# An attention and MLP kernel: MLP products as four of 32 columns, and scores in runs of three

## The chip, the core and the metric

The kernel runs on one core of a Trainium2 chip. TensorE (PE) multiplies, ScalarE (ACT) computes the exponentials and tanh, VectorE (DVE) does the elementwise work, GpSimd (POOL) and SyncE (SP) start most of the remaining transfers. The metric is the device time of one execution in microseconds, the median of a few runs.

## What is computed

From `x` (1, 2048, 640): a layer norm without weights, then two branches on it, multi-head attention (32 heads of 20 columns) and an MLP (640 to 1536 to 640, tanh gelu), both added to `x`.

```python
xn = _layernorm(x, axis=-1)
return x + _A_ref(xn, A_wqkv, A_wo) + _B_ref(xn, B_w1, B_b1, B_w2, B_b2)
...
scores = jnp.einsum("bhqd,bhkd->bhqk", q, k) * (Dh ** -0.5)
p = _softmax(scores, axis=-1)
o = jnp.einsum("bhqk,bhkd->bhqd", p, v)
...
y = _layernorm(x, axis=-1)
h = _gelu(jnp.einsum("bsd,df->bsf", y, w1) + b1)
return jnp.einsum("bsf,fd->bsd", h, w2) + b2
```

## The kernel before

All is computed in float32 accuracy from 16-bit pieces: an operand is split into a high and a low half, and a product is three passes (high by high, high by low, low by high; `PASS`).

**Stages.** First the norm, the transposes, the projections to queries, keys and values, and the splitting of the weights (up to 224 us). Then one long loop over attention, with the MLP laid between its parts, and at the end the output projection, whose first products also go into the loop when the results they need are there.

**The loop.** Heads go in pairs `g` (16 of them), the tokens of the queries in halves `hf` and quarters `cc` of 512 columns, the keys in 16 blocks `kb` of 128. `ORDER` runs through 32 pairs (g, hf); the last four g go through hf 0 first and hf 1 afterwards. For each key block:

- `scores` (L742, the products recorded at L748): two products, one for each head of the pair, with 61 rows each, at rows 0 and 64 of the array, into a PSUM tile `s` of 128 x 1024. The pool `psS` has three such tiles. ScalarE's exponential (L750) reads it and writes `p` in float32; `p` has seven buffers, `low` four.
- Half of the key blocks (`SPLIT` is 1, 1, 0, 0 and so on) have their values in 16-bit pieces. For these `rest` (L757) has VectorE subtract the upper half of `p` from `p` (L762), into `low` in f16; the value products then read the upper half as bf16, and `low`. For the other blocks `p` is multiplied as it is, in f32.
- `pv` (L767) does the value products, of 32 columns each (`product`, L778 and L779). Four quarters `q` of the array's columns write to four strips of 32 partitions of `o`. They accumulate over 16 key blocks; then ScalarE copies `o` to `ev` (L800).

**The order in the loop.** A group is four key blocks. It is written out by hand: scores of two blocks, a part of the MLP, scores of two blocks, the value products of the group before (the scores of the next two blocks follow). `tick` (L689) lets every side job (gelu, the sums behind the attention, loads) take one step after each run of two. `other` (L1186) doles out the MLP: each call adds `rate` = 1.265 us to a credit, and a unit of the MLP is cut in as many parts as its cost asks for.

**The MLP.** `chain` gives units: `layer1` (L1021, products at L1031: weights 128 x 128, 256 moving columns; a unit has 30, for two of the 12 blocks of hidden features) and `layer2` (L1053, products at L1061: 128 x 128 with 320 moving columns; 36 in a unit). They write to `psM`, one PSUM buffer, which the projection `z` (L1146) uses too. After a layer-1 unit `gelu` (L961) runs over several ticks: two VectorE steps, a third, ScalarE's tanh (L977), and three more on VectorE, which write `hT`.

**The end.** `finish` (L861) sums the two parts of a group of heads, divides by the sums and writes `oscr`. For the last heads it goes a shorter way: the sums are spread with small products `rb` (L931), and VectorE multiplies and splits (L942 to L944). `projection` (L1121) loads a piece of 256 tokens from `oscr` (`load_piece`, L1089) when all heads of these tokens are written (`known`), then does 15 products for each 128 tokens and 320 columns. After the loop, `more` (L1233) goes on with the projection, a tick after every three products.

Of the kernel before, what the change touches and what calls it, by code (L numbers as in the profile page):

```python
# [34 lines left out]
CHUNK = 1.75  # L35
# [9 lines left out]
def mha_mlp_kernel(tc, x, wqkv, wo, w1, b1, w2, b2, out):  # L45
# [4 lines left out]
    with (  # L50
# [617 lines left out]
        with ExitStack() as scope:  # L668
# [72 lines left out]

            def scores(g, hf, cc, kb):  # L742
# [24 lines left out]
            def pv(units):  # L767
# [240 lines left out]
            xs, hTs = {}, {}  # L1008
            unscaled = []
# [11 lines left out]
            def layer1(mc, f):  # L1021
# [4 lines left out]
                for i in range(2):  # L1026
                    n = 0
                    fo_ = (f + i) % 4 * P
                    for k in range(KD):
                        for a, b in PASS:  # L1030
                            nc.tensor.matmul(ps[:, i], w1v[:, k, (f + i) // 4, a, fo_ : fo_ + P], xnt[:, k, b, :],  # L1031
                                             start=(n == 0), stop=(n == 3 * KD - 1))
# [20 lines left out]
            def layer2(mc, j, hf):  # L1053
# [5 lines left out]
                for f in range(KF):  # L1059
                    for a, b in PASS:  # L1060
                        nc.tensor.matmul(ps[:, :320], hTs[mc][:, f, a, j * P : (j + 1) * P],  # L1061
                                         w2v[:, f, b, hf * 320 : (hf + 1) * 320],
                                         start=(n == 0), stop=(n == 3 * KF - 1))
# [112 lines left out]
            with tc.manual_schedule():  # L1176
# [3 lines left out]
                rate = 1.265  # L1180
                groups = [(g, hf, cc, kb) for g, hf in ORDER for cc in range(2) for kb in range(0, NKB, GRP)]
                prev = None

                runs = []

                def other():  # L1186

                    nonlocal credit
                    if not runs:
                        unit = next(fill)  # L1190
                        if unit is None:
                            credit = 0.0
                            return
# [6 lines left out]
                for g, hf, cc, kb0 in groups:  # L1200
                    units = []
                    for kb in range(kb0, kb0 + GRP):
                        units.append([g, hf, cc, kb, scores(g, hf, cc, kb)])
                        if kb % 2 == 0:
                            continue
                        reading[0] = kb % GRP > 1 and prev is not None and prev[-1][3] == NKB - 1
                        tick()
                        if kb % GRP == 1:

                            rest(units[0])
                            credit += rate
                            other()
                        else:
                            for u in units[1:]:
                                rest(u)
                            if prev:
                                pv(prev)
                            else:  # L1220

                                credit += rate
                                other()
                    prev = units
# [21 lines left out]
                pv(prev)  # L1246
# [96 lines left out]
```

## Time and profile before

| | us |
|---|---|
| median of three runs | 1337.81 (1336.13 to 1339.84) |
| span of the profiled execution | 1337.9 |
| loop, first score product to the last | 224.7 to 1270.5 |
| PE busy | 1325.8 |
| ACT busy | 1128.0 |
| DVE busy | 1055.1 |

The page lists busy time by engine, the share of it in 40 slices of the span, the chain of work that ended last, and the costliest groups of instructions. In a row of groups stand line, engine, operation, tiles, shapes and count, then busy time in us and the mean of one in ns, then the engine's idle time before them and who ended it. In a row of the timeline stand the start, the time from the first start to the last end, and the count of instructions merged into it; TensorE's products overlap, so the time that a block holds the engine is read from start to start. `q` behind an engine's name marks its queue, where it issues transfers.

### The profile page before, as it was taken

The numbers are of one execution on the slowest core, as the hardware profiler recorded it, in microseconds if no ns is written. First come the engines' busy times: TensorE is split into PE (matmuls) and PEld (weight loads), VectorE is DVE, ScalarE is ACT, GpSimd is POOL, SyncE is SP. The second block draws the span as 40 slices with busy tenths as digits, with TensorE's granted clock in tenths as the row PEclk, the third lists the DMA queues.
The fourth block names the chain that finished last, engine by engine and source line by source line (L and its number), as shares of the span: only waits on it lengthen the run. The fifth ranks groups of instructions, "written<-read, shape, count | busy, mean of one in ns | idle before, by whom it ended". The sixth has DMA issues, their size and how long they took to land.

```text
span 1337.9 us, 29042 instructions
## 1 busy us (share of the span) xinstructions
PE 1325.8 (99%) x11635; PEld 586.7 (44%) x11635; DVE 1055.1 (79%) x1431; ACT 1128.0 (84%) x1306; POOL 37.5 (3%) x86
## 2 busy tenths in 40 slices
PE   9999899999999999999999999999999999999998
PEld 6645456444434343434343443344443434333366
DVE  7656754998788989878897879888879888997742
ACT  7844334999999999999999999999999999999900
POOL 3010000000000000000000000000000000000000
PEclk9999899999999999999999999999999999999999
DMA  9778723021203232212322132223032323334375
GB/s 279 254 196 176 136 79 104 15 59 39 66 28 103 61 83 81 63 48 59 111 63 81 33 93 66 75 69 94 19 80 71 93 66 87 118 95 118 105 218 188
DMA packets 100326, 129.54 MB, mean 97 GB/s; under 512 B 24292, under 2 KB 66664, under 8 KB 100188
## 3 DMA queue, kind: packets, MB, share of 16 engines
q1 hardware_dynamic: 96652, 120.25, 31.6%
q0 software_dynamic: 2912, 6.90, 2.8%
q8 instruction: 92, 1.51, 0.5%
q10 hardware_dynamic: 624, 0.51, 0.1%
q14 instruction: 46, 0.38, 0.1%
HBM read 82.14 MB, written 42.51 MB: 93 GB/s over the span
## 4 chain that ended last, share of the span: by engine, by line
PE 87%; DVE 6%; DMA 4%; ACT 1%; issue 1%; SPq 0%; ACTq 0%; DVEq 0%
PE o L779 30%; PE s L748 20%; PE py L1061 13%; PE pu L1031 11%; PE z L1146 5%; PE qkp L337 5%; PE vp L410 3%; DVE low L762 2%; DMA xt<-in_A_x_dram 1%; DMA xnt<-row 1%; DMA qkscr<-qkhl 1%; DVE st L255 1%; DVE qkhl L353 1%; ACT p L750 1%; DMA wos<-in_A_wo_dram 0%
## 5 line engine op out<-in xcount | busy, mean ns | idle before, releaser
L750 ACT ACTIVATE p<-s 128x1024 f32<-128x1024 f32 x1024 | 973.9, 1050 | 33.1 <-PE s L748 27.1
L762 DVE TENSOR_TENSOR low<-p 128x1024 f16<-128x1024 f32 x512 | 614.3, 1218 | 144.8 <-ACT p L750 144.0
L779 PE MATMUL o<-p,vfull 128*32 128x512 bf16 (+1 forms) x4096 | 429.0, 493 | 0.0
L748 PE MATMUL s<-qs,ks 61*128 61x512 f16 x2048 | 311.4, 381 | 0.2 <-ACT p L750 0.2
L748 PEld LDWEIGHTS <-ks 61*128 61x128 f16 x2048 | 61.2, 94 | 278.4 <-issue 276.1
L1061 PE MATMUL py<-w2t,hT 128*128 128x320 f16 x1152 | 178.5, 300 | 0.0
L1031 PE MATMUL pu<-xm,w1t 128*128 128x256 f16 x1440 | 178.2, 273 | 0.1
L1031 PEld LDWEIGHTS <-w1t 128*128 128x128 f16 x1440 | 131.0, 98 | 64.0 <-issue 50.2
L1061 PEld LDWEIGHTS <-hT 128*128 128x128 f16 x1152 | 102.3, 98 | 88.1 <-issue 53.9
L337 PE MATMUL qkp<-xnt,wv 128*128 128x512 f16 x600 | 131.1, 379 | 1.3 <-issue 1.3
L779 PEld LDWEIGHTS <-vfull 128*32 128x32 f16 x3072 | 59.9, 95 | 138.4 <-issue 106.9
L779 PE MATMUL o<-low,vfull 128*32 128x512 f16 x1024 | 101.3, 377 | 0.1
L337 PEld LDWEIGHTS <-wv 128*128 128x128 f16 x600 | 58.2, 98 | 71.0 <-issue 1.6
L779 PEld LDWEIGHTS o<-p,vfull 128*32 128x32 f32 x2048 | 61.7, 108 | 53.2
L410 PE MATMUL vp<-wv,xnt 128*128 128x320 f16 x480 | 69.5, 306 | 3.7 <-DVE qkhl L353 3.7
L1146 PE MATMUL z<-w1t,ot 128*128 128x320 f16 x480 | 67.4, 299 | 0.0
L352 ACT ACTIVATE qkhl<-qkp,qks 128x1024 f16<-128x1024 f32 (+1 forms) x24 | 23.1, 964 | 46.3 <-PE qkp L337 26.6
L410 PEld LDWEIGHTS <-xnt 128*128 128x128 f16 x480 | 47.9, 100 | 23.8 <-issue 3.7
L1146 PEld LDWEIGHTS <-ot 128*128 128x128 f16 x480 | 46.0, 98 | 22.9 <-issue 5.5
L353 DVE SCALAR_TENSOR_TENSOR qkhl<-qkp,qks,qkhl 128x1024 f16<-128x1024 f32 (+1 forms) x24 | 26.5, 1104 | 32.9 <-ACT qkhl L352 32.9
L1103 DVE SCALAR_TENSOR_TENSOR acc<-z,sc,acc 128x320 f32<-128x320 f32 x32 | 17.5, 549 | 37.3 <-PE z L1146 37.2
L800 ACT ACTIVATE ev<-o 128x512 f32<-128x512 f32 x64 | 39.5, 618 | 2.2 <-PE o L779 2.1
(195 smaller groups left out, 670.4 us busy)
## 6 DMA issues: line engine op xcount, KB each, us to landing
qkscr<-qkhl SPq DMA_DIRECT2D x40, 256.0 KB
opart<-ev SPq DMA_DIRECT2D x124, 80.0 KB
ks<-qkscr SPq DMA_DIRECT2D x120, 80.0 KB
qs<-qkscr SPq DMA_DIRECT2D x192, 40.0 KB
oa<-opart SPq DMA_DIRECT2D x32, 240.0 KB
xt<-in_A_x_dram SPq DMA_DIRECT2D x16, 320.0 KB
xscr<-xnt SPq DMA_DIRECT2D x4, 1280.0 KB
xm<-xscr SPq DMA_DIRECT2D x8, 640.0 KB
```

The lines of the kernel that those rows point to most:

```text
L337: nc.tensor.matmul(ps[:, i, :], wv[:, k, q, a, mm * P : (mm + 1) * P], xnts[c][:, k, b, :], start=(k + n == 0), stop=(k == KD - 1 and n == 2))
L352: nc.scalar.activation(hl[:, 0, i0:i1], ps[:, i0:i1], AF.Copy, scale=a)
L353: nc.vector.scalar_tensor_tensor(hl[:, 1, i0:i1], ps[:, i0:i1], a, hl[:, 0, i0:i1], ALU.mult, ALU.subtract)
L410: nc.tensor.matmul(ps[:, hf, :320], xnts[c][:, k, a, j * P : (j + 1) * P], wv[:, k, 2, b, hf * 320 : (hf + 1) * 320], start=(n == 0), stop ...
L748: nc.tensor.matmul(ps[:, a, :], ks[64 * a : 64 * a + 61, kb * P : (kb + 1) * P], qs[64 * a : 64 * a + 61, cc * 512 : (cc + 1) * 512], star ...
L750: nc.scalar.activation(pt, ps, AF.Exp, scale=QS)
L762: nc.vector.tensor_sub(low, pt, upper(pt))
L779: nc.tensor.matmul(pv.o[32 * q : 32 * q + 32, :], src[:, v0 - PAD * (1 - q % 2) :][:, :32], t, start=q not in pv.begun, stop=last, skip_gr ...
L800: nc.scalar.activation(evs[g, hf][:, cc], pv.o, AF.Copy)
L1031: nc.tensor.matmul(ps[:, i], w1v[:, k, (f + i) // 4, a, fo_ : fo_ + P], xnt[:, k, b, :], start=(n == 0), stop=(n == 3 * KD - 1))
L1061: nc.tensor.matmul(ps[:, :320], hTs[mc][:, f, a, j * P : (j + 1) * P], w2v[:, f, b, hf * 320 : (hf + 1) * 320], start=(n == 0), stop=(n == ...
L1146: nc.tensor.matmul(ps[:, :320], ot[:, k, a, j * P : (j + 1) * P], wov[:, k, b, h * 320 : (h + 1) * 320], start=(n == 0), stop=(n == 3 * KD ...
```

## The change

1. The products of both MLP layers go through `quarters`: each product of 128 columns becomes four of 32 columns, one per strip of 32 output partitions, with the same moving operand. The projection's products stay as they are.
2. The loop goes over sets of eight key blocks. Scores come in runs of three, three and two. After each run comes a part of the MLP, and right behind it value products: after the first run those of the last four key blocks of the set before, after the second those of blocks 0 and 1, after the third those of blocks 2 and 3.
3. `other` is called after each run, with the shares 0.65, 1.46 and 0.52 us, and cuts a unit accordingly, at whole steps (three products of layer 1 or of the projection, two of layer 2).
4. `pv` does the f32 blocks before the split ones, not after.
5. `rest` is called after the first run for blocks 0 and 1, after the third for blocks 4 and 5; after the second run `tick` is called a second time. A gelu that isn't done when the next begins is run to its end first (`latest`).

```diff
-CHUNK = 1.75
+RUNS = (3, 3, 2)
+SHARE = (0.65, 1.46, 0.52)
...
+            def quarters(o, w, t, **kw):
+
+                for r in range(0, P, 32):
+                    nc.tensor.matmul(o[r : r + 32], w[:, r : r + 32], t, skip_group_check=True, **kw)
...
                 of32 = lambda kb, a: PAD + kb * VROW + (2 * g + a) * VW
+                for a in range(2):
+                    for n, (kb, pt) in enumerate(whole):
+                        product(2 * a + n % 2, vfull, of32(kb, a), pt[:, a])
                 for kb, up, _ in split:
...
-                for a in range(2):
-                    for n, (kb, pt) in enumerate(whole):
-                        product(2 * a + n % 2, vfull, of32(kb, a), pt[:, a])
...
-                            nc.tensor.matmul(ps[:, i], w1v[:, k, (f + i) // 4, a, fo_ : fo_ + P], xnt[:, k, b, :],
-                                             start=(n == 0), stop=(n == 3 * KD - 1))
+                            quarters(ps[:, i], w1v[:, k, (f + i) // 4, a, fo_ : fo_ + P], xnt[:, k, b, :],
+                                     start=(n == 0), stop=(n == 3 * KD - 1))
...
-                                    begin(gelu(ps, r2f, hTs[mc], f))
+                                    if latest and latest[0] in sides:
+                                        sides.remove(latest[0])
+                                        for _ in latest[0]:
+                                            pass
+                                    latest[:] = [gelu(ps, r2f, hTs[mc], f)]
+                                    begin(latest[0])
...
-                        nc.tensor.matmul(ps[:, :320], hTs[mc][:, f, a, j * P : (j + 1) * P],
-                                         w2v[:, f, b, hf * 320 : (hf + 1) * 320],
-                                         start=(n == 0), stop=(n == 3 * KF - 1))
+                        quarters(ps[:, :320], hTs[mc][:, f, a, j * P : (j + 1) * P],
+                                 w2v[:, f, b, hf * 320 : (hf + 1) * 320],
+                                 start=(n == 0), stop=(n == 3 * KF - 1))
...
-                rate = 1.265
...
+                    credit += SHARE[turnno % 3]
                     if not runs:
...
-                        k = max(round((cost - credit) / rate) + 1, math.ceil(cost / CHUNK))
-                        runs.extend(n * (i + 1) // k - n * i // k for i in range(k))
+                        lens = []
+                        have = credit
+                        while not lens or (cost - have > 0.5 * SHARE[(turnno + len(lens)) % 3] and len(lens) < n):
+                            if lens:
+                                have += SHARE[(turnno + len(lens)) % 3]
+                            lens.append(have)
+                        lens = [max(0.0, v) for v in lens]
+                        cuts = [round(n * v / lens[-1]) for v in lens] if lens[-1] > 0 else [n]
+                        runs.extend(y - x for x, y in zip([0] + cuts, cuts))
...
+                flow = [(g, hf, cc, kb0) for g, hf in ORDER for cc in range(2) for kb0 in range(0, NKB, 8)]
+                held = []
+                for g, hf, cc, kb0 in flow:
                     units = []
-                    for kb in range(kb0, kb0 + GRP):
-                        units.append([g, hf, cc, kb, scores(g, hf, cc, kb)])
...
+                    for r, n in enumerate(RUNS):
+                        for _ in range(n):
+                            kb = kb0 + len(units)
+                            units.append([g, hf, cc, kb, scores(g, hf, cc, kb)])
+                        reading[0] = r == 0 and kb0 == 0 and bool(held)
                         tick()
...
+                        other()
+                        if r != 1:
+                            for u in units[4:6] if r else units[:2]:
+                                rest(u)
                         else:
...
+                            reading[0] = False
+                            tick()
+                        if r == 0:
+                            if held:
+                                pv(held)
+                        else:
+                            pv(units[2 * r - 2 : 2 * r])
+                    held = units[4:]
```

More of the change, by code (lines that the diff above doesn't have):

```diff
@@ L1008, in mha_mlp_kernel @@
             xs, hTs = {}, {}
+            latest = []
             unscaled = []
@@ L1179, in mha_mlp_kernel @@
                 credit = 0.0 - next(fill)
-                rate = 1.265
-                groups = [(g, hf, cc, kb) for g, hf in ORDER for cc in range(2) for kb in range(0, NKB, GRP)]
-                prev = None
                 runs = []
+                turnno = 0
                 def other():
-                    nonlocal credit
+                    nonlocal credit, turnno
+                    credit += SHARE[turnno % 3]
                     if not runs:
@@ L1197, in other @@
+                        lens = [max(0.0, v) for v in lens]
+                        cuts = [round(n * v / lens[-1]) for v in lens] if lens[-1] > 0 else [n]
+                        runs.extend(y - x for x, y in zip([0] + cuts, cuts))
                     for _ in range(runs.pop(0)):
                         credit -= next(fill)
-                for g, hf, cc, kb0 in groups:
+                    turnno += 1
+                flow = [(g, hf, cc, kb0) for g, hf in ORDER for cc in range(2) for kb0 in range(0, NKB, 8)]
@@ L1207, in mha_mlp_kernel @@
                         tick()
[L1208 to L1214, printed above, removed]
-                        else:
[L1216 to L1223, printed above, removed]
```

7 lines of the change are left out of this document (2 added, 5 removed).

## The prediction

> **What bounds the kernel now.** I read the page first: the span, the busy shares, the chain that ended last.
>
> ```profile
> span 1337.9 us, 29042 instructions
> PE 1325.8 (99%) x11635; PEld 586.7 (44%) x11635; DVE 1055.1 (79%) x1431; ACT 1128.0 (84%) x1306; POOL 37.5 (3%) x86
> PE 87%; DVE 6%; DMA 4%; ACT 1%; issue 1%; SPq 0%; ACTq 0%; DVEq 0%
> L750 ACT ACTIVATE p<-s 128x1024 f32<-128x1024 f32 x1024 | 973.9, 1050 | 33.1 <-PE s L748 27.1
> ...
> L748 PE MATMUL s<-qs,ks 61*128 61x512 f16 x2048 | 311.4, 381 | 0.2 <-ACT p L750 0.2
> ```
>
> TensorE carries the chain. The average hides stages, so next came the loop alone, from the first score product to the last (busy times by stretch: length, then PE, PEld, DVE, ACT, POOL, each with its count, then the granted clock):
>
> ```profile
> 224.70:1271.00 1046.30, 1045.89 (x9791) 419.75 (x9794) 892.66 (x1064) 1013.00 (x1134) 13.58 (x16) 1.00 0.26 72
> ```
>
> PE has no gap in 1046 us; ScalarE is at 97% of it. A gain on PE is thus worth its full size only until ScalarE stands in the way. How PE spends the loop, and what ScalarE needs, shows in the timeline:
>
> ```profile
> 602.84 0.60 PE L748 MATMUL s<-qs,ks 61*128 61x512 f16 x4
> 603.38 1.16 PE L1031 MATMUL pu<-xm,w1t 128*128 128x256 f16 x9
> 604.47 0.61 PE L748 MATMUL s<-qs,ks 61*128 61x512 f16 x4
> 605.00 0.64 PE L779 MATMUL o<-p,vfull 128*32 128x512 bf16 x8
> 605.47 0.39 PE L779 MATMUL o<-low,vfull 128*32 128x512 f16 x4
> 605.68 1.03 PE L779 MATMUL o<-p,vfull 128*32 128x512 f32 x8
> 606.64 0.60 PE L748 MATMUL s<-qs,ks 61*128 61x512 f16 x4
> ...
> 611.01 1.48 PE L1031 MATMUL pu<-xm,w1t 128*128 128x256 f16 x12
> 612.43 0.60 PE L748 MATMUL s<-qs,ks 61*128 61x512 f16 x4
> ...
> 624.06 1.26 PE L1061 MATMUL py<-w2t,hT 128*128 128x320 f16 x8
> 625.25 0.61 PE L748 MATMUL s<-qs,ks 61*128 61x512 f16 x4
> ...
> 627.97 1.53 PE L1061 MATMUL py<-w2t,hT 128*128 128x320 f16 x10
> 629.43 0.61 PE L748 MATMUL s<-qs,ks 61*128 61x512 f16 x4
> ```
>
> ```profile
> 603.27 3.77 ACT L750 ACTIVATE p<-s 128x1024 f32<-128x1024 f32 x4 [0.17 <-PE s L748]
> 606.90 0.63 ACT L800 ACTIVATE ev<-o 128x512 f32<-128x512 f32 x1
> 607.38 7.49 ACT L750 ACTIVATE p<-s 128x1024 f32<-128x1024 f32 x8
> ```
>
> From start to start, 9 products of layer 1 hold PE 1.09 us (603.38 to 604.47) and 12 hold it 1.42. Three more cost 0.33, so 0.109 each, and 1.09 - 9 x 0.109 = 0.107 is a fixed price of the block. Layer 2: 1.19 for 8, 1.46 for 10, so 0.135 each and 0.11 over. A run of two key blocks' scores takes 0.54, again 0.107 plus 2 x 0.216. Inside the value products, which change from bf16 to f16 to f32, the steps of 0.46, 0.21 and 0.96 hold one such price, at the end (0.96 = 0.855 + 0.107). So PE pays 0.107 us whenever the shape of the array's tiles changes, not when the type does. For ScalarE: four exponentials in 603.27 to 606.90, so 0.907 us apart, 1.05 long; the first starts 0.43 after its run of scores does.
>
> **The change, part by part.**
>
> *Changes of shape.* By the order of the built programs, the loop before has 1023 blocks of one shape on PE (512 of scores, 254 of value products, 257 of the MLP and projection); the changed one has 792 (384 of scores, 383 of 32 columns, 25 of projection, which stays 128 wide). 231 blocks x 0.107 = **-24.7 us**.
>
> *Quarters.* 1440 + 1152 products become four each, so 7,776 more matmuls and as many weight loads. What a quartet costs is shown by the one other place of this shape with short moving rows:
>
> ```profile
> 56.22 0.52 PE L382 MATMUL norms<-sq,heads 128*32 128x128 bf16 x24
> 56.67 1.09 PE L299 MATMUL pt<-ident,xt 128*128 128x128 f32 x8
> ...
> 93.19 0.41 PE L382 MATMUL norms<-sq,heads 128*32 128x128 bf16 x16
> 93.52 0.39 PE L114 MATMUL mxp<-acc,ones 128*128 128x5 f32 x2
> ```
>
> 24 of them hold PE 0.45 us, 16 hold it 0.33: eight more take 0.12 (a rounding of 0.01 either way), so a quartet with 128 columns takes 0.055 to 0.065, loads included, and one with 256 should take 0.11, as the whole product does. The 16-bit value quartet (605.47, 0.21 for 512 columns) says the same. The bf16 quartets (0.46 for two) are 0.015 dearer; at that price 2592 quartets would add 39 us. I take 0: the MLP's operands lie dense in 16 bits, as those of the 0.21 row do. Ends: -5 and +39.
>
> *Three score buffers, runs of three.* The scores' tiles still rotate through three buffers. With runs of two, the second key block of a run waits for an exponential of an earlier run that ended long ago. With runs of three, the third block waits for the last exponential of the run before (after a run of two, too). With t the start of a run of three, m the MLP time in a run: its last exponential ends at t + 0.43 + 2 x 0.907 + 1.05 = t + 3.29. PE reaches the next run's third block at t + 0.755 (three blocks of scores) + m + 1.64 (f32 0.855, bf16 0.465, f16 0.215, change 0.107) + 0.43. So PE waits if m is under 0.47 in the first run of a set of eight key blocks, and by the same sum (0.54 + m + 0.96 + 0.43 against 0.43 + 0.907 + 1.05) if m is under 0.46 in the third. In the second run, with its shorter value products, m under 1.18 makes ScalarE late by the difference. The built program's chunks, over 128 sets: first run 0.52 to 0.81 in 116, 0.33 or less in 6; third run 0.54 in 47, 0.65 in 42, 0.33 or less in 19; second run 1.31 or more in 106. These small chunks cost 19 x 0.14 + 6 x 0.14 and 21 sets with a light second run some 3: together 6.5 us. Then the 48 tanh, which ScalarE runs between exponentials:
>
> ```profile
> L977 ACT ACTIVATE w<-w 128x512 f32<-128x512 f32 x48 | 32.0, 666 | 0.0
> L800 ACT ACTIVATE ev<-o 128x512 f32<-128x512 f32 x63 | 38.9, 618 | 0.1
> L966 DVE TENSOR_TENSOR u<-pu,r2f 128x512 f32<-128x512 f32 x48 | 32.8, 683 | 0.2
> ```
>
> A tanh takes 0.52 of ScalarE's time (0.666 less the 0.14 by which exponentials overlap, 1.05 - 0.907). Twenty stand behind a second run: the next exponentials are late by 1.18 + 0.52 - 1.33 = 0.37, of which the third run's spare (0.54 or 0.65 less 0.46) hides 0.14; 20 x 0.23 = 4.6. Nineteen stand behind a third run, where most is hidden: 1.5; nine behind a first: 0.5. The 63 copies of o (0.48) fall where ScalarE waits for PE anyway: 0. Sum of waits **+13 us**; ends 0 (where a wait already taken relieves the next, and more is hidden) and +28 (a slower hand-over, below).
>
> *VectorE and the single buffer of the MLP.* A unit's first product waits until VectorE has read the unit before (0.68, L966). PE's time between the MLP parts of two runs shrinks from at least 2.7 (604.47 to 607.18) to 0.465 + 0.215 + 0.107 + 0.54 = 1.33 after a second run. Latency and 0.68 fit if VectorE, 85% busy in the loop, is free: some 40 ends of units x 0.05, **+2 us**; ends 0 and 8. The sums and lows that are moved wait on nothing new that is late: the latest `low` is emitted in the third run and used at the end of the next first run, over 4 us on.
>
> *The tail.* The shares add up to 2.63 per eight blocks, where 2 x 1.265 were given before, so the loop takes 165 projection products, not 66. That work is only moved. But these are the rows of the first half of the tokens, which now cover the wait for the last heads:
>
> ```profile
> 1274.99 9.55 PE L1146 MATMUL z<-w1t,ot 128*128 128x320 f16 x69
> ...
> 1284.46 2.50 PE L931 MATMUL rb<-lt,sel 64*80 64x64 f32 x32
> ...
> 1286.90 39.70 PE L1146 MATMUL z<-w1t,ot 128*128 128x320 f16 x291
> ...
> 1288.80 0.67 DVE L942 TENSOR_TENSOR oa<-oa,rb 80x512 f32<-80x512 f32 x1
> ...
> 1290.69 2.10 ACTq L945 DMA_DIRECT2D oscr<-oa  x2
> ...
> 1293.98 1.03 SPq L1097 DMA_DIRECT2D ot<-oscr  x2
> ```
>
> Before, 339 products follow `rb` (291 + 48), 99 of them of the first half: 13.6 us of cover. In the changed order 240 follow, all of the second half: no cover. What is late then: VectorE's three steps (1288.80 to 1290.69, 1.9), the write of `oscr` until its reader may start (to 1293.98, 3.3), the load of `ot` (two of 320 KB: landed by 1300.5, when PE uses it without a wait, so 1.03 to 6.5; I take 4.4). PE stands still for 9.6 us, and then the clock drops, as it did here:
>
> ```profile
> 159.50 1.76 PE L410 MATMUL vp<-wv,xnt 128*128 128x320 f16 x6 [3.67 <-DVE qkhl L353]
> 158.10:164.90 6.80, 5.40 (x21) 3.08 (x21) 6.43 (x16) 0.72 (x1) 0.00 (x0) 0.50 0.75 178
> ```
>
> A gap of 3.7 us led to 5.4 us of work at half clock, 2.7 lost. Together **+12.3 us**; ends +6 and +15.
>
> *Sum.* -24.7 + 0 + 13 + 2 + 12.3 = +2.6, of which I take off 1 because waits of the ring and of VectorE partly fall together: 1337.9 + 1.6 = **1339.5 us**, against the profiled execution's span, which is that of the median (1337.81). The measurement tells 0.3% (4 us) from no change.
>
> **Rivals.**
>
> *Faster.* The ring hardly waits, since each wait gives the next runs slack, and `ot` lands early: -24.7 + 3 + 0 + 9 = -12.7, **1325 us**. For it: ScalarE's own need in the loop is 1024 x 0.907 + 48 x 0.52 + 63 x 0.48 = 984 us, 37 less than the 1021 left to PE. Against: slack in the mean does not help a run whose buffer is taken.
>
> *The ring locks.* Place: the third scores of every run of three. The margins above are 0.07 to 0.19 us, at a hand-over from ScalarE to PE taken as zero. From 0.15 us on, the 78 runs with chunks of 0.54 wait too, and all others longer: some 16 us more, **1356 us**. For it: PE waited only 0.2 us for ScalarE in the loop before, so no row shows the hand-over. Against: the exponential's 1.05 may contain it.
>
> *PE's instruction supply.* The loop then issues 9791 + 7776 = 17,567 matmuls in 1,020 us, 58 ns each, where before it was 107. Place: PE's queue, in the MLP parts. It decides from the point where PE's instruction stream gives a matmul and its load less often than every 58 ns; each ns more costs 17.6 us, so 3 ns add 53: with the tail's 12 **1403 us**. The rows bound it only loosely: 24 pairs in 0.45 us (a burst that can have waited in a queue) on the one side, 107 ns and +860 us on the other; I take the burst's side. [...]
>
> *The change does not do what it says:* the quarters run one after another, 7,776 x 0.109 = +850 us. The rows of `norms` speak against it.
>
> **How the numbers follow.** Forecast 0.45 (its own range 1331 to 1348: 0.09 faster, 0.19 within 0.3%, 0.17 slower); faster 0.28; the ring locks 0.15; supply 0.10; in series 0.02. Faster 0.09 + 0.28 = 0.37, same 0.19, slower 0.44. The range reaches from the best ends (-24.7 + 0 + 6 + waits of 3) to the ring that locks with some dearer quartets: 1321 to 1360; supply and series, 0.12, and a part of the edges are left out.
>
> **What would show it.** Right: fewer and longer blocks on PE, 0.11 us per layer-1 quartet; some 10 us of waits of `s` on ScalarE where before were 0.2; one gap of 8 to 11 us behind `rb` and a second stretch at clock 0.5. Wrong: a quartet above 0.12 (or gaps on PE that nothing but issue ends) raises the time at once, 2.6 us for each ns; no waits of `s` and a short gap give the faster case; a loop that is no shorter than 1046 us with few waits would say that the fixed price of a change of shape is not what 0.107 stood for.

## The result, and the profile after

Measured side by side on one chip, the changed kernel takes 1369.61 us (median of four runs, 1366.91 to 1371.94) where the kernel before takes 1338.45 (four runs): a ratio of 1.0236, 95% interval 1.0206 to 1.0266. It is 2.4% slower. The profiled execution's span is 1369.9 us, 32.0 more than before. The forecast was 1339.5 us, with 1360 as the upper end.

The page of the changed kernel, the same parts as before:

```profile
span 1369.9 us, 44648 instructions
PE 1327.5 (97%) x19411; PEld 645.9 (47%) x19411; DVE 1056.9 (77%) x1431; ACT 1131.1 (83%) x1306; POOL 37.7 (3%) x86
PE 63%; DVE 16%; ACT 9%; DMA 6%; issue 4%; SPq 1%; ACTq 0%; DVEq 0%
L756 ACT ACTIVATE p<-s 128x1024 f32<-128x1024 f32 x1024 | 971.6, 1040 | 60.9 <-PE s L754 55.2
...
L754 PE MATMUL s<-qs,ks 61*128 61x512 f16 x2048 | 298.9, 381 | 8.7 <-ACT p L756 7.3
...
L746 PE MATMUL py<-w2t,hT 128*32 128x320 f16 x4608 | 190.5, 302 | 8.0 <-DVE u L972 5.0
L746 PE MATMUL pu<-xm,w1t 128*32 128x256 f16 x5760 | 190.3, 274 | 0.7 <-DVE u L972 0.6
...
L785 PE MATMUL o<-low,vfull 128*32 128x512 f16 x1024 | 111.1, 378 | 5.0 <-DVE low L768 4.8
...
L1158 PE MATMUL z<-w1t,ot 128*128 128x320 f16 x480 | 72.4, 305 | 8.0 <-DMA ot<-oscr 8.0
L972 DVE TENSOR_TENSOR u<-pu,r2f 128x512 f32<-128x512 f32 x48 | 33.1, 690 | 57.1 <-PE pu L746 56.2
```

Every engine is busy for as long as before (DVE 1056.9 against 1055.1, ACT 1131.1 against 1128.0), so the span did not grow by busy time; it grew by waiting. TensorE now waits in four kinds of places where it hardly waited before: the scores for ScalarE, `low` and the MLP for VectorE, `z` for a transfer. In the chain, VectorE went from 6% to 16% and ScalarE from 1% to 9%. The last row is a hint: VectorE stands idle for 56 us in front of the gelu's first step, whose products TensorE hasn't finished (before, in the row of L966, 0.2), and what is queued behind that step on VectorE waits along.

The blocks themselves are as long as forecast. From the timeline of TensorE in the middle of the loop:

```profile
604.05 1.54 PE L746 MATMUL py<-w2t,hT 128*32 128x320 f16 x40
...
605.41 0.63 PE L785 MATMUL o<-p,vfull 128*32 128x512 bf16 x8
...
611.41 0.82 PE L754 MATMUL s<-qs,ks 61*128 61x512 f16 x6
...
612.16 1.49 PE L746 MATMUL pu<-xm,w1t 128*32 128x256 f16 x48
...
613.48 0.62 PE L785 MATMUL o<-p,vfull 128*32 128x512 bf16 x8
```

Ten products of layer 2, 40 quarters, hold TensorE for 1.36 us from start to start (10 x 0.135 = 1.35, with no price of a change, since value products of the same shape follow). Twelve of layer 1, 48 quarters, hold it for 1.32, so 0.110 each (0.109 before). A run of three key blocks' scores takes 0.75. What TensorE computes in the loop is thus as short as forecast. The loop is not:

```profile
223.00:1305.00 1082.00, 1059.65 (x17671) 488.50 (x17673) 896.72 (x1070) 1015.60 (x1134) 13.78 (x16) 1.00 0.27 74
```

The columns are those of the loop's row in the prediction. From the first to the last score product it is 1081.9 us where it was 1045.8: 36.1 more, of which 13.4 are the 99 projection products that moved into it. TensorE has 22 us of idle time in it. The idle time counts from the modelled end of the product before; what a wait costs is read from start to start. Over all neighbouring products of the loop I took that distance less the usual one of their kind:

| us that TensorE lost | forecast | before | after |
|---|---|---|---|
| third scores of a run (before: second), waiting for ScalarE | 13 | 1.2 | 18.2 (72 times) |
| value products, waiting for `low` | 0 | 1.9 | 15.9 (44 times) |
| first product of an MLP unit, waiting for VectorE to read the MLP's buffer | 2 | 0.2 | 9.5 (10 times) |
| stretches at half clock in the loop | 0 | 0 | 4.3 |
| tail: gaps behind `rb`, and half clock | 12.3 | 0 | 10.0 |

With the -24.7 of the changes of shape and the 5.9 us that the loop before lost by the same count (the three shown and 2.6 between f32 value products), the sum is -24.7 + 18.2 + 15.9 + 9.5 + 4.3 + 10.0 - 5.9 = +27.3 of the 32.0 us. Another 1.9 is what quarters alone add to the loop (run e1 below). Some 3 us, in the loop, have no place in this account.

How `low` comes late shows in a timeline of the changed kernel (a stretch in which a second run begins at 287.93):

```profile
285.75 0.72 PE L746 MATMUL pu<-xm,w1t 128*32 128x256 f16 x20
285.94 0.68 DVE L985 SCALAR_TENSOR_TENSOR u<-w,u 128x512 f32<-128x512 f32 x1
...
287.18 0.75 DVE L987 SCALAR_TENSOR_TENSOR hT<-u,sc,hT 128x512 f16<-128x512 f32 x1
...
287.93 0.86 PE L754 MATMUL s<-qs,ks 61*128 61x512 f16 x6
...
288.04 0.69 DVE L972 TENSOR_TENSOR u<-pu,r2f 128x512 f32<-128x512 f32 x1
...
288.65 2.35 DVE L768 TENSOR_TENSOR low<-p 128x1024 f16<-128x1024 f32 x2
...
288.78 0.84 PE L746 MATMUL pu<-xm,w1t 128*32 128x256 f16 x24
...
289.43 0.64 PE L785 MATMUL o<-p,vfull 128*32 128x512 bf16 x8
...
289.91 0.38 PE L785 MATMUL o<-low,vfull 128*32 128x512 f16 x1
...
291.05 0.40 PE L785 MATMUL o<-low,vfull 128*32 128x512 f16 x3 [0.76 <-DVE low L768]
```

VectorE took its instructions in the order of the program. The unit's last products were done at 286.5 (285.75 + 0.72), but the gelu before had three steps left, which came first (285.94 to 287.93). Then VectorE read `pu` (288.04), and only then came the two `low` (1.2 us each), from 288.65 to 291.00. TensorE's part of the MLP in this run was short (288.78 to 289.43); it came to the second `low` at about 290 and stood until 291.05.

And how the MLP's buffer comes late, the dearest case:

```profile
433.33 0.68 ACT L983 ACTIVATE w<-w 128x512 f32<-128x512 f32 x1
...
434.05 0.69 DVE L985 SCALAR_TENSOR_TENSOR u<-w,u 128x512 f32<-128x512 f32 x1 [1.52 <-ACT w L983]
434.77 0.49 DVE L986 TENSOR_SCALAR hT<-u,sc 128x512 f16<-128x512 f32 x1
435.30 0.75 DVE L987 SCALAR_TENSOR_TENSOR hT<-u,sc,hT 128x512 f16<-128x512 f32 x1
436.15 0.69 DVE L972 TENSOR_TENSOR u<-pu,r2f 128x512 f32<-128x512 f32 x1
...
436.89 0.72 PE L746 MATMUL py<-w2t,hT 128*32 128x320 f16 x8 [3.12 <-DVE u L972]
...
437.38 1.94 PE L785 MATMUL o<-p,vfull 128*32 128x512 f32 x8
```

Here the gelu before wasn't done when a unit ended, and `latest` ran it to its end first. VectorE waited 1.52 us for its tanh, did the three steps behind it, and only then read `pu`; TensorE, whose next unit needs that buffer, stood for 3.1 us. Then the f32 value products took 1.94 us instead of 1.03. The granted clock says why (by stretch, in the columns of the loop's row; two lie in the loop, one in the tail):

```profile
435.76:442.59 6.83, 5.70 (x46) 1.73 (x49) 6.62 (x9) 2.77 (x4) 0.00 (x0) 0.50 0.00 0
1186.70:1190.11 3.41, 2.81 (x24) 0.91 (x23) 3.38 (x7) 0.00 (x0) 0.00 (x0) 0.50 0.19 46
1323.23:1333.47 10.24, 3.95 (x15) 1.99 (x16) 1.95 (x4) 0.00 (x0) 0.00 (x0) 0.50 0.77 227
```

Two of the loop's waits (3.1 us, and 2.7 at 1184.56) were each followed or overlapped by a stretch at half clock. TensorE worked for 5.70 and 2.81 us of these stretches (the second column), and half of that is the 4.3 of the table.

The wait at 1184.56 has another cause than the rest of its row. It hangs on VectorE's sum of a layer-2 unit into `xb` (L1003), and that sum on a transfer (the second line is from the list of transfers, with the time from issue to landing):

```profile
1181.00 1.02 POOL L1063 DMA_DIRECT2D xb<-in_B_b_dram  x1 [64.74 <-DMA xb<-in_A_x_dram]
xb<-in_B_b_dram POOLq DMA_DIRECT2D x1, 320.0 KB, 5.6
...
1186.70 0.55 DVE L1003 SCALAR_TENSOR_TENSOR xb<-py,sc,xb 128x320 f32<-128x320 f32 x1 [3.10 <-issue]
...
1187.30 1.26 PE L746 MATMUL py<-w2t,hT 128*32 128x320 f16 x16 [2.74 <-DVE xb L1003]
```

The load of `xb` landed at 1186.6 and the sum began at 1186.70. The profile's row names no releaser, but the times fit this load. In the kernel before, the same load landed at 1185.7 and its sum ran only at 1191.9. So 2.8 of the 9.5 us, and the stretch at half clock behind them, come from a transfer that the new order asks for sooner.

The third stretch belongs to the tail:

```profile
1319.07 2.50 PE L937 MATMUL rb<-lt,sel 64*80 64x64 f32 x32
...
1329.17 0.71 PE L1158 MATMUL z<-w1t,ot 128*128 128x320 f16 x2 [7.60 <-DMA ot<-oscr]
1330.23 5.96 PE L1158 MATMUL z<-w1t,ot 128*128 128x320 f16 x31 [0.35 <-DMA ot<-oscr]
```

The gap behind `rb` is 7.6 us (forecast 9.6), and 0.35 more go to the second part of the load. Of the 10.24 us at half clock TensorE worked 3.95; half of that, 2.0, is lost (forecast 2.7).

### The profile page after: what moved, and what is told of

Same layout as the page of the kernel before. It is cut to its first block, busy times and chain, and to the rows that moved or that the text cites. A ratio compares the mean times of both kernels' runs of the same rounds, so it can differ in the third digit from the quotient of the medians.

```text
span 1369.9 us, 44648 instructions
## 1 busy us (share of the span) xinstructions
PE 1327.5 (97%) x19411; PEld 645.9 (47%) x19411; DVE 1056.9 (77%) x1431; ACT 1131.1 (83%) x1306; POOL 37.7 (3%) x86
## 4 chain that ended last, share of the span: by engine, by line
PE 63%; DVE 16%; ACT 9%; DMA 6%; issue 4%; SPq 1%; ACTq 0%; DVEq 0%
PE o L785 20%; PE s L754 13%; PE pu L746 9%; PE py L746 9%; DVE low L768 7%; ACT p L756 7%; PE z L1158 5%; PE vp L411 3%; PE qkp L338 3%; DMA xnt<-row 1%; DMA xt<-in_A_x_dram 1%; DVE u L972 1%; DMA qkscr<-qkhl 1%; DVE w L976 1%; DVE qkhl L354 1%
## 5 line engine op out<-in xcount | busy, mean ns | idle before, releaser
L768 DVE TENSOR_TENSOR low<-p 128x1024 f16<-128x1024 f32 x512 | 599.8, 1217 | 52.7 <-ACT p L756 52.2
L785 PE MATMUL o<-p,vfull 128*32 128x512 bf16 (+1 forms) x4096 | 405.4, 493 | 0.0
L754 PE MATMUL s<-qs,ks 61*128 61x512 f16 x2048 | 298.9, 381 | 8.7 <-ACT p L756 7.3
L754 PEld LDWEIGHTS <-ks 61*128 61x128 f16 x2048 | 83.6, 94 | 268.7 <-issue 234.2
L746 PE MATMUL py<-w2t,hT 128*32 128x320 f16 x4608 | 190.5, 302 | 8.0 <-DVE u L972 5.0
L746 PE MATMUL pu<-xm,w1t 128*32 128x256 f16 x5760 | 190.3, 274 | 0.7 <-DVE u L972 0.6
L746 PEld LDWEIGHTS <-w1t 128*32 128x32 f16 x5760 | 137.2, 96 | 68.1 <-issue 65.3
L785 PEld LDWEIGHTS <-vfull 128*32 128x32 f16 x3072 | 87.0, 97 | 139.9 <-issue 104.1
L746 PEld LDWEIGHTS <-hT 128*32 128x32 f16 x4608 | 107.8, 96 | 94.3 <-issue 71.0
L972 DVE TENSOR_TENSOR u<-pu,r2f 128x512 f32<-128x512 f32 x48 | 33.1, 690 | 57.1 <-PE pu L746 56.2
```

What stands on the lines that cost most here:

```text
L746: nc.tensor.matmul(o[r : r + 32], w[:, r : r + 32], t, skip_group_check=True, **kw)
L754: nc.tensor.matmul(ps[:, a, :], ks[64 * a : 64 * a + 61, kb * P : (kb + 1) * P], qs[64 * a : 64 * a + 61, cc * 512 : (cc + 1) * 512], star ...
L768: nc.vector.tensor_sub(low, pt, upper(pt))
L785: nc.tensor.matmul(pv.o[32 * q : 32 * q + 32, :], src[:, v0 - PAD * (1 - q % 2) :][:, :32], t, start=q not in pv.begun, stop=last, skip_gr ...
L972: nc.vector.tensor_mul(u, ps, r2f[:, None, :].to_broadcast([P, 2, MC]))
```

## The experiments

Twelve variants ran. The last three columns are TensorE's losses in the loop by the count above.

| run | us | ratio to before (95%) | loop | ScalarE | `low` | MLP buffer |
|---|---|---|---|---|---|---|
| changed kernel | 1369.61 | 1.0236 (1.0206 to 1.0266) | 1081.9 | 18.2 | 15.9 | 9.5 |
| e1_quarters_only | 1339.2 | 1.0017 (0.9995 to 1.0038) | 1047.7 | 1.1 | 2.0 | 0.2 |
| e2_lows_first | 1411.53 | 1.0561 (1.0512 to 1.0611) | 1123.6 | 14.4 | 1.0 | 60.4 |
| e4_tail_cover | 1354.54 | 1.0136 (1.0099 to 1.0173) | 1068.9 | 24.3 | 17.3 | 4.9 |
| e7_whole | 1391.61 | 1.0424 (1.0388 to 1.0461) | 1100.8 | 8.0 | 9.1 | 6.6 |
| e5_one_low_first | 1356.86 | 1.0144 (1.0118 to 1.0171) | 1066.3 | 25.5 | 4.1 | 11.0 |
| e6_no_tanh | 1335.92 | 0.9988 (0.9971 to 1.0005) | 1049.4 | 14.4 | 11.8 | 1.4 |
| e8_gelu_stepped | 1417.72 | 1.0613 (1.0562 to 1.0663) | 1128.4 | 14.7 | 84.7 | 0.2 |
| e9_pool | 1398.41 | 1.0449 (1.0421 to 1.0478) | 1110.5 | 17.3 | 63.8 | 6.8 |
| e10_short_gelu | 1327.82 | 0.9922 (0.9894 to 0.995) | 1037.9 | 14.6 | 1.5 | 0 |
| e11_shares_low | 1360.87 | 1.017 (1.0117 to 1.0223) | 1075.6 | 23.0 | 8.7 | 12.5 |
| e12_sums_pool | 1370.31 | 1.0249 (1.0223 to 1.0275) | 1083.6 | 22.9 | 33.3 | 4.8 |
| e13_both_pool | 1389.06 | 1.0388 (1.0364 to 1.0413) | 1103.2 | 27.6 | 44.2 | 5.5 |

### Quarters in the loop of before

```diff
-nc.tensor.matmul(ps[:, i], w1v[:, k, (f + i) // 4, a, fo_ : fo_ + P], ...
+quarters(ps[:, i], w1v[:, k, (f + i) // 4, a, fo_ : fo_ + P], ...
-nc.tensor.matmul(ps[:, :320], hTs[mc][:, f, a, j * P : (j + 1) * P], ...
+quarters(ps[:, :320], hTs[mc][:, f, a, j * P : (j + 1) * P], ...
```

> The kernel before with the MLP's products as quarters, nothing else changed (runs of two, same order). The MLP part still stands between two runs of scores, so no change of the array's shape is saved. Theory W (the change loses by waits, a quartet costs what a whole product does): same as before, 1338 us within 5. Rival S (7,776 more matmuls and loads cost time by themselves, in the weight loads or in PE's instruction supply): 1350 us or more, with layer-1 quartets above 0.115 us from start to start.

Ratio 1.0017, an interval that holds 1. The loop of this kernel by the view of stretches:

```profile
223.00:1273.00 1050.00, 1049.63 (x17584) 443.51 (x17586) 892.88 (x1064) 1013.76 (x1135) 13.59 (x16) 1.00 0.26 73
```

17,584 recorded products in 1049.63 us are 59.7 ns each, without a gap on TensorE. The loop is 1.9 us longer than before (1047.7 against 1045.8), under 1 ns for each of the 2592 quartets. Quarters cost next to nothing, and the rival of the instruction supply falls. A block of 48 quarters of layer 1, 1.32 us in the changed kernel (above), comes to 27.5 ns each, less than half of the 58 from which that rival counts.

### The whole change without quarters

```diff
-quarters(ps[:, i], w1v[:, k, (f + i) // 4, a, fo_ : fo_ + P], ...
+nc.tensor.matmul(ps[:, i], w1v[:, k, (f + i) // 4, a, fo_ : fo_ + P], ...
-quarters(ps[:, :320], hTs[mc][:, f, a, j * P : (j + 1) * P], ...
+nc.tensor.matmul(ps[:, :320], hTs[mc][:, f, a, j * P : (j + 1) * P], ...
```

> The changed kernel with whole MLP products of 128 columns, all else as changed (runs of three, same order). 1149 blocks of one shape where the changed kernel has 792: 357 more changes of shape. Theory W: 357 x 0.107 = 38 us more on PE, of which part falls into waits that are there already: 1385 to 1408 us. Rival S (the quarters themselves cost time): faster than the changed kernel or the same, under 1372 us.

1391.61, as expected. The loop has 1149 blocks of one shape in this order, 357 more than with quarters: at 0.107 us that is +38 us. The three kinds of waits fall by 20, and the 4.3 us of half clock are gone. That leaves +14, and the loop grew by 18.9, so a change of shape cost here somewhat more than 0.107. A part of it shows in the timeline: f32 value products right behind a whole product of the MLP hold TensorE for 1.00 us (602.12 to 603.12 in this run), behind quarters for 0.96 (607.40 to 608.36 in the changed kernel). So the changes of shape are worth at least what the prediction said, and waits eat half of it as soon as they are saved.

### The `low` ahead of the gelu

```diff
-                        tick()
-                        other()
                         if r != 1:
                             for u in units[4:6] if r else units[:2]:
                                 rest(u)
-                        else:
+                        tick()
+                        other()
+                        if r == 1:
                             reading[0] = False
```

> The changed kernel with the subtractions of `low` emitted before the tick and the MLP part of the same run, not behind them. Theory W: VectorE's queue is what makes the value products wait (some 16 us between two products of `low`); these waits fall under 5 us, the wait for the MLP's buffer may grow by a few: 1352 to 1364 us. Rival R (the ring of three score buffers makes everything late, VectorE only follows): no change, 1366 us or more.

The waits for `low` went (15.9 to 1.0), as expected, but the time, expected at 1352 to 1364, rose by 42 us. In the groups of this kernel in its loop:

```profile
L746 PE MATMUL py<-w2t,hT 128*32 128x320 f16 x4608 | 193.2, 305 | 30.1 <-DVE u L972 25.8 <-DVE xb L1003 4.3
L746 PE MATMUL pu<-xm,w1t 128*32 128x256 f16 x5736 | 190.8, 275 | 23.7 <-DVE u L972 15.0 <-DVE xb L1003 8.7
```

Two `low` (2.4 us) now stand in front of the read of the MLP's buffer, and the first products of units wait for it: 60.4 us, and eight stretches at half clock in the loop. VectorE's order trades one wait for the other, and the order that the change chose is the cheaper of the two.

### Cover for the tail

```diff
-SHARE = (0.65, 1.46, 0.52)
+SHARE = (0.62, 1.43, 0.50)
```

> The changed kernel with shares of 0.62, 1.43 and 0.50 in place of 0.65, 1.46 and 0.52, so that the loop takes 87 projection products, not 165, and 75 products of the first half stand behind `rb` as cover. Prediction's account of the tail: the gap of 7.6 us behind `rb` and the half clock after it (10 us, so 5 lost) go: 9 to 13 us less, 1357 to 1361 us; the waits in the loop stay within 6 us. Rival (the work moved back costs what the gap did, because it filled waits in the loop): 1366 us or more.

Smaller shares leave 75 projection products behind `rb`. The gap there is gone (the group of `z` has 0.0 idle, where after has 8.0), and 1354.54 is 15 us less than the changed kernel. 10 of these are the tail's; most of the rest comes from the loop, where the two 3-us waits and their half clock (4.3) didn't occur. Its sum of the three waits, 46.5, is no smaller. This is the best of the variants that compute everything in the changed order, still 1.4% behind the kernel before.

### One `low` ahead, on top of it

```diff
+                        if r == 2:
+                            rest(units[4])
                         tick()
+                        if r == 0:
+                            rest(units[0])
                         other()
                         if r != 1:
-                            for u in units[4:6] if r else units[:2]:
-                                rest(u)
+                            rest(units[5] if r else units[1])
```

> e4 (smaller shares, 1354.5 us) with only the first `low` of a pair emitted earlier: in the first run behind the tick but ahead of the MLP part, in the third ahead of the tick; the second `low` stays behind the MLP part. Theory V (VectorE's queue is too short of time: what is put first makes the other late): the waits between the products of `low` (17 us in e4) halve, but the waits for the MLP's buffer (5 us) grow by about as much; 1347 to 1362 us. Rival (order alone is at fault and this order is right): low waits under 5 us and buffer waits no more than in e4: 1340 to 1346 us.

No gain against e4: the waits for `low` fall by 13, those for the MLP's buffer rise by 6, those for ScalarE by 1, and two stretches at half clock come back (3.4). The same trade, in small.

### Without the tanh, and without most of the gelu

Both on e4. e6 leaves out the 48 tanh. e10 leaves out the tanh and four of VectorE's steps around it (the bias, the square, the step behind it and the first behind the tanh), and with them the ticks between, so that only the read of `pu` and the two writes of `hT` remain.

```diff
-                nc.scalar.activation(w, w, AF.Tanh, scale=0.7978845608028654 * 0.044715)
...
-                nc.vector.tensor_add(u, u, b1t[:, f : f + 2, None].to_broadcast([P, 2, MC]))
-                nc.vector.tensor_mul(w, u, u)
-                nc.vector.scalar_tensor_tensor(w, w, 1.0 / 0.044715, u, ALU.add, ALU.mult)
-                nc.vector.scalar_tensor_tensor(u, w, 1.0, u, ALU.add, ALU.mult)
```

> e4 with the 48 tanh of ScalarE left out (the gelu goes on with its argument in place of the tanh). In e4, PE's scores wait 24 us for exponentials, 12 of them in runs behind a tanh. Theory (the ring of three buffers has no room for a tanh): these 12 us go, the 17 us of waits for `low` stay above 12: 1340 to 1347 us. Rival (ScalarE is late because of what VectorE does): the waits of the scores stay above 20 us, 1350 us or more.

> e6 with, besides the tanh, the four VectorE steps left out that feed and follow it (bias, square, cube, product; some 130 us of VectorE's 895 in the loop): the gelu is only scaled and split. Theory V (VectorE's queue is short of time, and the ring adds its own): the waits for `low` and the MLP's buffer, 13 us in e6, fall under 3; the scores' waits of 14 us stay above 8, since they come from chunks that are too small: 1320 to 1329 us. Rival (the low waits come from VectorE standing in front of a sum of the MLP that PE has not ended, which stays): low waits 9 us or more, 1332 us or more.

The tanh alone is worth 18.6 us, more than expected (the waits for `low` were to stay above 12): 10 of waits for ScalarE, 5.5 for `low` and 3.5 for the MLP's buffer, though only 32 us of ScalarE's 1014 went. A tanh between two exponentials delays both the third scores and everything that VectorE has queued behind it (at 433.33, above, VectorE stood for 1.52 us in front of the tanh, and TensorE behind it for 3.1). With the four steps gone as well, waits on VectorE are 1.5 us in all:

```profile
L754 PE MATMUL s<-qs,ks 61*128 61x512 f16 x2048 | 297.6, 380 | 5.7 <-ACT p L756 4.6
L746 PE MATMUL pu<-xm,w1t 128*32 128x256 f16 x5760 | 191.2, 274 | 0.0
L746 PE MATMUL py<-w2t,hT 128*32 128x320 f16 x4608 | 190.3, 301 | 0.0
...
L785 PE MATMUL o<-low,vfull 128*32 128x512 f16 x1024 | 101.2, 377 | 0.2 <-DVE low L768 0.2
```

Now the order of the change is faster than the kernel before, by 0.8%. Its loop can be worked out: 1045.8 - 24.7 (shapes) + 14.6 + 1.5 (waits) - 5.9 (what the loop before lost) + 2.8 (21 projection products more than before) = 1034.1; measured are 1037.9, and 1.9 of the difference are the quarters' (e1). The saving was there all along, and the waits behind the gelu hid it. Run e10 takes away 109 us of VectorE's work and the places of these steps in its order at once; which of the two counts more it doesn't show. That ScalarE still costs 14.6 shows that VectorE isn't all of it.

### A step of the gelu earlier

```diff
+                        if r != 1 and latest and latest[0] in sides:
+                            if next(latest[0], self_end) is self_end:
+                                sides.remove(latest[0])
                         reading[0] = r == 0 and kb0 == 0 and bool(held)
```

> e4 with one extra step of the running gelu at the start of each first and third run, so that no gelu has to be run to its end when the next begins (7 of 48 had to in e4). Theory V: only the waits that hang on a gelu that is still running go (some of the 5 us for the MLP's buffer): 1348 to 1356 us. Rival (the gelu that is late is behind the waits for `low` too): low waits under 8 us, 1346 us or less.

This, too, is on e4. It did what it was for: no gelu is run to its end in a hurry, and the MLP's buffer costs 0.2 us. But the steps now reach VectorE before what they need is there (VectorE's largest groups in the loop):

```profile
L768 DVE TENSOR_TENSOR low<-p 128x1024 f16<-128x1024 f32 x512 | 600.2, 1218 | 62.8 <-ACT p L756 62.1 <-issue 0.2
...
L985 DVE SCALAR_TENSOR_TENSOR u<-w,u 128x512 f32<-128x512 f32 x48 | 33.1, 689 | 44.7 <-ACT w L983 44.7
```

VectorE stands for 44.7 us in front of a tanh that ScalarE has not reached (in e4 21.3), with `low` queued behind it: 84.7 us of waits. The expectation of a gain was wrong; it counted the steps that get done early and not those issued too early.

### Relief for VectorE by GpSimd

Three tries: e9 is e5 with the step of e8 and the square on GpSimd; e12 is e4 with two of the four steps of each sum behind the attention there; e13 is e12 with the square as well.

```diff
-                nc.vector.tensor_mul(w, u, u)
+                nc.gpsimd.tensor_tensor(w, u, u, ALU.mult)
...
-                    nc.vector.tensor_add(o0, o0, o1)
+                    nc.gpsimd.tensor_tensor(o0, o0, o1, ALU.add)
-                    nc.vector.tensor_mul(o0, o0, rb)
+                    nc.gpsimd.tensor_tensor(o0, o0, rb, ALU.mult)
```

> e5 and e8 together, and one of the gelu's VectorE steps (the square of u, 48 times 0.69 us) moved to GpSimd. Theory V (VectorE's time is what is short): 33 us less work on VectorE takes more off the waits of `low` and of the buffer than order did: 5 to 12 us below the better of e5 and e8. Rival (VectorE's time is not short, or GpSimd's step is slower and the gelu's chain longer by it): no better than they.

> e4 with two of the four steps of each group's sum behind the attention (the add and the multiply of `oa`, 22 of each, 0.685 us) on GpSimd in place of VectorE. Nothing on TensorE waits for them soon. That takes 30 of the 893 us that VectorE works in the loop; leaving out 109 and the tanh took the waits on VectorE from 22 to 2 us, leaving out the tanh alone from 22 to 13. Theory (VectorE's load sets these waits): 30/109 of the 11 us that the steps alone were worth, and less in the second order, so 3 us off e4's 1354.5: 1349 to 1353. Rival (the place of single steps in VectorE's order sets them, not its load): 1354 to 1358, and the add now ties up GpSimd for 1 us each time, which nothing waits for.

> e12 with the square of u (48 of 0.69 us) on GpSimd too, where one took 1.04 us. VectorE has 63 us less of work than in e4. Theory (load): 63/109 of 11 us, so 6 us off e4: 1346 to 1350, still behind the kernel before. Rival (order): VectorE's next step needs the square and stands in its queue until GpSimd has it (1.04 us and two hand-overs in place of 0.69), with `low` behind it: some 48 x 0.5 us late on VectorE, of which a third shows on TensorE, so 1358 to 1366.

All three are slower than what they were to improve; e9 beats e8 alone, by 19 us. In e12 neither theory holds. From its page, and a stretch of its timeline:

```profile
PE 1331.9 (97%) x19411; PEld 649.9 (47%) x19411; DVE 1064.6 (78%) x1387; ACT 1129.5 (82%) x1306; POOL 109.7 (8%) x130
L768 DVE TENSOR_TENSOR low<-p 128x1024 f16<-128x1024 f32 x512 | 630.5, 1278 | 53.6 <-ACT p L756 53.1
```

```profile
1051.51 1.27 POOL L956 TENSOR_TENSOR oa<-oa 120x512 f32<-120x512 f32 x1 [21.71 <-DMA oa<-opart]
1051.74 4.34 DVE L768 TENSOR_TENSOR low<-p 128x1024 f16<-128x1024 f32 x2
...
1052.97 2.03 POOL L958 TENSOR_TENSOR oa<-oa,rb 120x512 f32<-120x512 f32 x1 [0.19 <-DMA qs<-qkscr]
...
1056.14 0.40 PE L785 MATMUL o<-low,vfull 128*32 128x512 f16 x3 [1.55 <-DVE low L768]
```

44 instructions of 0.685 us left VectorE, and it is busy 8 us longer than in e4 (1056.6). Two `low` that met GpSimd took 4.34 us where a pair takes 2.35; the 43 that overlapped one of its steps took 1.92 each on average, the others 1.22. A `low`, which reads `p` and the upper half of `p`, took up to 2.96 us, so it is late by up to 1.74, the length of a step of GpSimd (1.59 and 1.76 on average for the two kinds); the gelu's first step, with one input from PSUM, took 0.69 in all five places where it met GpSimd. So moving these sums to GpSimd relieved VectorE of nothing; why the two engines hold each other up, no run shows. The square is another matter. In e9 it meets no step of VectorE, whose busy time falls by 31 us (1025.9 against 1056.6 in e4), but VectorE's next step stands for it longer than that:

```profile
L978 DVE SCALAR_TENSOR_TENSOR w<-w,u 128x512 f32<-128x512 f32 x48 | 33.2, 692 | 58.5 <-POOL w L976 58.5
```

e13, with both, came out above the two ranges that were expected.

### Other shares

```diff
-SHARE = (0.62, 1.43, 0.50)
+SHARE = (0.66, 1.33, 0.57)
...
+                        if r == 2:
+                            rest(units[4])
...
-                            for u in units[4:6] if r else units[:2]:
+                            for u in units[5:6] if r else units[:2]:
```

> e4 with shares of 0.66, 1.33 and 0.57 (66 products of cover) and, in the third run only, the first `low`, whose exponential is over by then, ahead of the tick. By the prediction's bounds on the chunks (0.47, 1.18 and 0.46 us) the chunks should cost 4 us of waits, where they cost 9 in e4; the waits for `low` in first runs (6.5 of 17 us) should go, without later sums for the MLP, since that `low` waits for nothing: 1342 to 1349 us. Rival (as in e5, each gain comes back as another wait): 1352 us or more.

On e4, 1360.87: the rival was right. `low` costs 8.7 instead of 17.3, but the MLP's buffer 12.5 instead of 4.9, with five stretches at half clock. Longer parts in the first and third runs didn't relieve the third scores either (23.0 against 24.3).

No variant that computes the whole result beats the kernel before.

## Why the prediction was wrong

*Changes of shape, -24.7: right.* The blocks last as computed (0.75, 1.32, 1.36), e7 pays at least 0.107 for each of its 357 more, and e10 shows the saving as time.

*Quarters, 0: right* within 2 us, shown alone by e1. The rival of the instruction supply added 3 ns for each matmul; no run shows them, and the 1.9 us of e1 are 0.1 ns for each.

*Three score buffers, +13: right in kind, too small.* 18.2 us (the upper end was 28). The third scores wait where the sum said, behind short parts of the MLP and behind the tanh, and it is the tanh that the sum made too small. Some 11 us fall on runs with a tanh among ScalarE's exponentials since the run before began, where the sum had 6.6; some 7 on the others, where it had 6.5. e6 takes 10 of e4's 24 away with the tanh. The rival in which the ring locks, at 1356, had some 29 us of waits; it came only in part, with 72 waits in 256 runs of three.

*The tail, +12.3: right in kind, a little too large.* 10.0 us, with a shorter gap (7.6 and 0.35 against 9.6) and less work at half clock (2.0 against 2.7); e4 takes it away.

*VectorE and the single buffer, +2: the step that failed.* The prediction said that the sums and `low` that are moved "wait on nothing new that is late: the latest `low` is emitted in the third run and used at the end of the next first run, over 4 us on". That looks at the `low` of blocks 4 and 5 alone; it left out those of blocks 0 and 1, made in the first run and used in the second, on which 11.4 of the 15.9 us fall; those of blocks 4 and 5 cost 4.6. And it asked whether VectorE is free on average (85% busy) instead of reading its queue in order. In the kernel before the first `low` of a group came ahead of `other`; in the order of the change every `low` stands behind what `tick` and `other` give VectorE, so behind the gelu's read of `pu`, and this behind the unit's last product or the steps of the gelu before. Together 15.9 us for `low` and 9.5 for the buffer where 2 stood, with ends of 0 and 8; of the 9.5, 2.8 are the late load of `xb`, which the sum didn't have either. Runs e2, e5, e8 and e11 show that no order of these few instructions that was tried frees both: in e5 and e11 most of what was taken from one wait came back in another or at half clock, in e2 and e8 several times as much. Runs e6 and e10 show the cause from the other side: without the tanh both waits fall, and with less gelu both go.

*Half clock in the loop: not in the sum.* The prediction priced it for the tail, from the row at 159.50, but not for waits in the loop, which it held to be short. 4.3 us.

The rival "faster" supposed that each wait gives the next runs slack, and put the ring's waits at 3 us; they are 18.2. What would have given the answer beforehand: VectorE's program order through one set of eight key blocks, each of its instructions with the time at which its input is ready.

Open stay three things: some 3 us of the loop have no place in the account; whether VectorE's amount of work or its order weighs more wasn't parted, since the tries with GpSimd brought waits of their own; and a second PSUM buffer for the MLP, which might part the two waits, wasn't tried.

## What to carry to other kernels

When a change makes the leading engine faster, walk the queues of the engines behind it in program order: ask of each instruction when its input is there and what stands behind it, not how busy the engine is on average. An instruction issued before its input is ready costs whatever is queued behind it, so a later place can be the cheaper one (waits for `low` of 84.7 us in e8, of 17.3 in e4, where the steps of the gelu come later). A buffer that is single was paced by the old order, and what is saved on TensorE (24.7 us here) is worth only the part that these buffers can follow.

## What the runs showed of the hardware

- 32-column quarters with a weight load each ran with hardly a loss through the loop of e1: 59.7 ns per matmul over 1050 us, 1.9 us more than with whole products. In the changed kernel a block of 48 took 27.5 ns for each.
- A wait of 2.7 us on TensorE came with half clock in the changed kernel: idle from 1184.56 to 1187.30, granted clock 0.50 from 1186.70 to 1190.11, and the 3.41 us ahead of 1186.70 held 2.1 of idle time. Its stretches were 3.41, 6.83 and 10.24 us long, multiples of one length. A wait of 1.2 us (e4, at 300.89) was followed by none; in e5 waits of 0.3 and 1.55 us close together stood ahead of a stretch that began at 568.64. Over the loops of all runs the 3.41 us ahead of each of 23 stretches held 1.8 to 3.2 us of idle time.
- The 43 `low` on VectorE that met one of GpSimd's two-tile steps on SBUF (e12) took 1.92 us on average, the others 1.22; these steps took 1.6 to 1.8 us on GpSimd, where VectorE needed 0.69 (e4).
